# Attention with grouped queries on one core: K of group 1 by transposed load, VectorE's share of the exponentials from chunk 3 to 381, first chunks in two exponentials, other orders of loads and stores

## Chip, cores and metric

One core of a Trainium2 chip. Times are microseconds (us) of one execution on the device; the median of several is quoted. A "look" is the one execution of a run that was profiled; a "hole" is time in which TensorE starts no matmul though it has work left.

## The reference

```python
B, Hq, Hkv, Sq, Sk, D = 16, 32, 8, 288, 512, 128      # q, k, v in bf16, normal * 0.05
k = jnp.repeat(k, 4, axis=1); v = jnp.repeat(v, 4, axis=1)
scores = jnp.einsum("bhqd,bhkd->bhqk", q, k) * D ** -0.5
out = jnp.einsum("bhqk,bhkd->bhqd", softmax(scores), v)
```

A group is one KV head with its four query heads: 128 groups, each 4 x 288 = 1152 query rows (9 tiles of 128) against 512 keys (4 tiles). Its 4608 score columns are cut into three chunks of 1536: 384 chunks.

## The kernel before

For each chunk n, TensorE computes the scores S into one of two PSUM halves, ScalarE the exponential into one of six SBUF buffers, and two chunks later TensorE the product with V (PV); VectorE takes a reciprocal of the row sum and multiplies. In every sixth chunk 120 columns are "shared": VectorE computes their exponential itself by a polynomial, in eight operations spread over two iterations.

```python
FIRST = 2; FIRST_SHARED = 6; EVERY = 6; LAG = 2; UG = 4; NSLOT = 3    # 4 groups are a unit of K and V
def shared(n): return FIRST_SHARED <= n < NS - NC and (n - FIRST_SHARED) % EVERY == 0    # NS 384, NC 3
# TensorE
for n in range(NS):
    op_s(n)                       # waits for K, for Q, and for the exponential of chunk n - 2
    if shared(n): op_sy(n)        # the 120 columns, into a free corner of PSUM
    if n == 2: op_kt(1, range(NJ), 1)     # K of group 1: four transposes on TensorE
    if n >= LAG: op_pv(n - LAG)   # waits for V, exponentials, and VectorE's eviction of r - 2
# VectorE
for r in range(NS - 1):
    n = r + LAG
    op_rc(r)
    if shared(n): op_y(n)
    if shared(n - 1): op_yu(n - 1, 1); op_yu(n - 1, 2); op_yp(n - 1)
    op_ev(r)
    if shared(n): op_yb(n); op_ym(n); op_yu(n, 0)
# GpSimd: V from its landing buffer to the layout for TensorE, one copy per group
def op_vc(g):    # waits: V landed; s_pv >= 3 * (g - 2) + 2
    tensor_copy(v_sb[...], vd_sb[...])
# SyncE: loads of the start, in order; the rest is a list sorted by due times
first = [q(0), v(groups 0), q(1), k(groups 2..3), v(groups 1..3), q(2), q(3)]
# ScalarE issues K of group 0 and, when that is in place, K of group 1 (both plain, for TensorE's transposes)
```

## Time and profile before

| | us |
|---|---|
| time, median of 6 runs (521.55 to 522.85) | 521.69 |
| span of the profiled run | 519.98 |
| first exponential / end of the last | 5.05 / 516.47 |
| six chunks in the steady part | 7.98 |
| scores of chunk 6 begin / its Q landed | 12.39 / 11.37 |

The lines that carry the reading are in the prediction. A timeline line is: start, duration, engine, line of the kernel, operation, output<-input, shape, count, and in brackets the idle time before it and what ended it. PE is TensorE, DVE VectorE, ACT ScalarE, POOL GpSimd, SPq SyncE's issues. L439 or L449 is S, L479 or L489 is PV (the changed kernel's lines lie 10 lower). Matmul ends are modelled, so a hole is read from starts. "The clock is full" is read from starts too: 512-column matmuls start 0.427 apart before it and 0.216 after it.

### The profile page before, as it was taken

The page shows a single profiled execution, that of the slowest core. Times are in us where ns is not written, and L with a number is a line of the kernel's source. Part 1 is how long each engine was busy: PE and PEld are TensorE (multiplying, and loading weights), DVE is VectorE, ACT ScalarE, POOL GpSimd, SP SyncE. Part 2 cuts the span into 40 slices and gives each one's busy share as a digit, 9 for nine tenths or more (in the row PEclk, how much of TensorE's full clock was granted, in tenths as well). Part 3 has the DMA queues.
Part 4 walks back from the last instruction along what each step waited for, and adds up shares of the span by engine and source line. Part 5 has one row for each costly group of instructions (what it writes and reads, how often), then busy time and mean ns, then how long its engine had stood idle before and what let it go on. Part 6 is the DMA issues. An engine that isn't in the chain of part 4 may idle for free.

```text
span 520.0 us, 15243 instructions
## 1 busy us (share of the span) xinstructions
PE 510.3 (98%) x6118; PEld 394.6 (76%) x6224; DVE 369.6 (71%) x1315; ACT 513.3 (99%) x393; POOL 79.8 (15%) x135
## 2 busy tenths in 40 slices
PE   8999999999999999999999999999999999999997
PEld 5777777777777777777777777777777777777776
DVE  2767767777777677676776776767767767677776
ACT  7999999999999999999999999999999999999997
POOL 2111111111111111111111111111111111111110
PEclk9999999999999999999999999999999999999999
DMA  9999999999999998999999989999998989998212
GB/s 186 237 218 230 267 194 248 225 213 210 219 233 256 208 245 201 235 248 240 215 241 209 209 225 220 241 185 209 229 240 232 227 194 201 192 234 198 86 69 93
DMA packets 253078, 110.06 MB, mean 212 GB/s; under 512 B 219728, under 2 KB 236752, under 8 KB 253008
## 3 DMA queue, kind: packets, MB, share of 16 engines
q1 hardware_dynamic: 252720, 108.82, 97.7%
q8 instruction: 49, 0.80, 0.7%
q10 hardware_dynamic: 288, 0.26, 0.2%
q14 instruction: 21, 0.17, 0.2%
HBM read 17.04 MB, written 37.75 MB: 105 GB/s over the span
## 4 chain that ended last, share of the span: by engine, by line
ACT 98%; DMA 1%; issue 1%; DVE 0%; PE 0%
ACT pt_sb L516 97%; DMA qt_sb<-in_q_dram 1%; ACT pt_sb L511 1%; PE ps_s L439 0%; DVE o_sb L585 0%; DVE o_sb L595 0%; PE ps_s L479 0%; DVE rl_sb L575 0%; PE ps_o L669 0%; DVE bad_sb L621 0%; DVE flag_i L734 0%; DVE bad_sb L618 0%
## 5 line engine op out<-in xcount | busy, mean ns | idle before, releaser
L516 ACT ACTIVATE pt_sb<-ps_s 128x1536 bf16<-128x1536 f32 (+2 forms) x384 | 508.8, 1441 | 0.0
L479 PE MATMUL ps_o<-v_sb,pt_sb 128*128 128x129 bf16 x4584 | 322.3, 220 | 1.1
L479 PEld LDWEIGHTS ps_o<-v_sb,pt_sb 128*128 128x128 bf16 x4584 | 282.8, 98 | 49.7 <-DVE o_sb L585 14.1
L439 PE MATMUL ps_s<-qt_sb,kt_sb 128*128 128x512 bf16 (+2 forms) x1430 | 290.4, 320 | 5.0 <-DMA qt_sb<-in_q_dram 0.5
L585 DVE TENSOR_TENSOR o_sb<-ps_o,rl_sb 128x384 bf16<-128x384 f32 x382 | 211.9, 555 | 9.3 <-DVE rl_sb L575 0.5
L439 PEld LDWEIGHTS ps_s<-qt_sb,kt_sb 128*128 128x128 bf16 x1536 | 123.9, 98 | 62.3 <-issue 1.1
L575 DVE RECIPROCAL rl_sb<-ps_o 128x3 f32<-128x3 f32 x382 | 68.1, 178 | 125.5 <-PE ps_o L479 124.0
L568 POOL COPY v_sb<-vd_sb 128x512 bf16<-128x512 bf16 x128 | 78.8, 616 | 429.1 <-PE ps_o L479 408.9
L549 DVE SCALAR_TENSOR_TENSOR u_sb<-u_sb,m_sb 128x120 f32<-128x120 f32 x126 | 35.6, 283 | 2.2
L556 DVE SCALAR_TENSOR_TENSOR pt_sb<-u_sb,e_sb 128x120 bf16<-128x120 f32 x63 | 17.8, 283 | 2.2
L549 DVE SCALAR_TENSOR_TENSOR u_sb<-m_sb 128x120 f32<-128x120 f32 x63 | 17.4, 277 | 0.0
L527 DVE TENSOR_SCALAR y_sb<-ps_o 128x120 f32<-128x120 f32 x63 | 15.9, 253 | 0.0
L540 DVE TENSOR_SCALAR m_sb<-t_sb 128x120 int32<-128x120 int32 x63 | 14.1, 223 | 2.2
L540 DVE TENSOR_SCALAR e_sb<-t_sb 128x120 int32<-128x120 int32 x63 | 13.6, 216 | 0.0
L450 PE MATMUL ps_o<-qt_sb,kt_sb 128*128 128x120 bf16 x63 | 13.6, 216 | 0.0
L533 DVE TENSOR_SCALAR t_sb<-y_sb 128x120 int32<-128x120 f32 x63 | 13.4, 213 | 0.0
L450 PEld LDWEIGHTS ps_o<-qt_sb,kt_sb 128*128 128x128 bf16 x63 | 6.2, 98 | 7.4
L511 ACT ACTIVATE pt_sb<-ps_s 128x512 bf16<-128x512 f32 x6 | 3.3, 616 | 2.3 <-PE ps_s L439 2.3
L411 DVE COPY kt_sb<-ps_o 128x128 bf16<-128x128 bf16 (+2 forms) x3 | 1.0, 336 | 6.2 <-PE ps_o L404 6.1
L613 DVE TENSOR_REDUCE st_sb<-rl_sb 128x1 f32<-128x72 f32 (+1 forms) x16 | 3.5, 216 | 0.0
L611 DVE TENSOR_REDUCE st_sb<-rl_sb 128x1 f32<-128x72 f32 (+1 forms) x16 | 3.5, 216 | 0.0
L417 PE MATMUL ps_o<-const-bfloat16-1.0 128*128 128x512 bf16 (+1 forms) x6 | 2.4, 570 | 0.9 <-PEq L752 0.9
(32 smaller groups left out, 12.0 us busy)
## 6 DMA issues: line engine op xcount, KB each, us to landing
out_dram<-o_sb SPq DMA_DIRECT2D x127, 288.0 KB, 3.7
vd_sb<-in_v_dram SPq DMA_DIRECT2D x31, 512.0 KB, 5.5
qt_sb<-in_q_dram SPq DMA_TRANSPOSE x128, 4.9
kt_sb<-in_k_dram SPq DMA_TRANSPOSE x32, 5.1
vd_sb<-in_v_dram SPq DMA_DIRECT2D x1, 384.0 KB, 4.6
out_dram<-o_sb SPq DMA_DIRECT2D x3, 96.0 KB, 1.6
kd_sb<-in_k_dram ACTq DMA_DIRECT2D x2, 128.0 KB, 2.7
vd_sb<-in_v_dram SPq DMA_DIRECT2D x1, 128.0 KB, 3.3
```

The lines of the kernel that those rows point to most:

```text
L439: ins = emit(eng, w_x, lambda: eng.matmul(ps_s[:, n % 2, c:c + w], kt_sb[:, sl, j, gi, :], qg[:, t * P:t * P + w], start=True, stop=True))
L450: emit(eng, [("s_ev", n - LAG - 1)], lambda: eng.matmul(ps_o[:, (n - LAG) % 2, BANK - W:BANK], kt_sb[:, (g // UG) % NSLOT, j, g % UG, :], ...
L479: ins = emit(eng, w_x, lambda: eng.matmul(outs(r)[:, t - r % NC * TPC, :], pt(g, t, j), v_sb[:, sl, gi * NJ + j, 0:DV], start=(x == 0), st ...
L516: emit(eng, waits, lambda: eng.activation(d, s, ACTF.Exp, scale=scale)).then_inc(sem["s_e"], 1)
L527: emit(eng, [("s_yb", nth(n) - NB), ("s_pv", n - LAG + 1)], lambda: eng.tensor_scalar(out=y_sb[:, b], in0=ps_o[:, (n - LAG) % 2, BANK - W: ...
L533: emit(eng, [("s_ym", 2 * (nth(n) - NB)), ("s_y", nth(n))], lambda: eng.tensor_scalar(out=t_sb[:, b], in0=y_sb[:, b], scalar1=Y_MUL, scala ...
L540: emit(eng, [("s_yp", nth(n) - NB), ("s_yb", nth(n))], lambda: eng.tensor_scalar(out=dst[:, b], in0=t_sb[:, b], scalar1=mask, scalar2=bits ...
L549: lambda: eng.scalar_tensor_tensor(out=u_sb[:, b, x], in0=src, scalar=QUARTIC[x], in1=m, op0=ALU.add, op1=ALU.mult)
L556: lambda: eng.scalar_tensor_tensor(out=pt_sb[:, n % NPT, CH - W:CH], in0=u_sb[:, b, 2], scalar=QUARTIC[3], in1=e_sb[:, b].bitcast(FP32), o ...
L568: emit(eng, waits, lambda: eng.tensor_copy(v_sb[:, sl, gi * NJ:(gi + 1) * NJ, 0:D], vd_sb[:, sl, gi].rearrange("p (j d) -> p j d", d=D))). ...
L575: emit(eng, [("s_pv", r + 1)], lambda: eng.reciprocal(rl_sb[:, TPC * r:TPC * (r + 1)].unsqueeze(2), outs(r)[:, :, D:DV])).then_inc(sem["s_ ...
L585: emit(eng, waits, lambda: eng.tensor_tensor(out=o_sb[:, g % NO, t0:t0 + TPC, :], in0=outs(r)[:, :, 0:D], in1=rl_sb[:, TPC * r:TPC * (r + ...
```

## The change

Its intent: take the four transposes of K of group 1 off TensorE's start, relieve ScalarE earlier and once more at the end, and loosen the first and last steps.

```diff
-    FIRST = 2
-    FIRST_SHARED = 6
+    FIRST = 3
+    PARTS = {0: (1, 2, 3), 1: (2, 3), 2: (2, 3), NG * NC - 1: (1, 2, 3)}   # where exponentials are cut, in banks of 512
+    FIRST_SHARED = 3
+    FINE = NG - 2                                   # groups stored chunk by chunk (was: the last alone)
-            return FIRST_SHARED <= n < NS - NC and (n - FIRST_SHARED) % EVERY == 0
+            return FIRST_SHARED <= n < NS - 2 and (n - FIRST_SHARED) % EVERY == 0
-        first += [lambda: op_q(1), lambda: op_k(0, 2), lambda: op_v(0, None, 1, UG), lambda: op_q(2), lambda: op_q(3)]
+        first += [lambda: op_q(1), lambda: op_k(0, 1, 2), lambda: op_v(0, None, 1, 2), lambda: op_k(0, 2), lambda: op_v(0, None, 2, UG), lambda: op_q(2), lambda: op_q(3)]
-            sp.append((t, lambda u=u: op_k(u)))
-            sp.append((t + (2.0 if u >= NSLOT else 0.35), lambda u=u: op_v(u)))
+            sp.append((t + (0.35 if u == 1 else 0), lambda u=u: op_k(u)))
+            sp.append((t + (2.0 if u >= NSLOT else 0 if u == 1 else 0.35), lambda u=u: op_v(u)))
-                if n == 2:
-                    op_kt(1, range(NJ), 1)
-            op_kd(eng, 1)                                # on ScalarE, after a wait
-            op_kc(1, range(NJ), 1, 3)                    # on VectorE
```

More of the change, by code (lines that the diff above doesn't have):

```diff
@@ L205, in bass_standalone__gqa_softmax__near_ridge_kernel @@
             S("s_k%d" % i)
-        for name in ["s_v0", "s_v1", "s_s0", "s_y", "s_yb", "s_ym", "s_yu", "s_yp", "s_kd0", "s_kd1", "s_id", "s_kp"]:
+        for name in ["s_v0", "s_v1", "s_v2", "s_s0", "s_y", "s_yb", "s_ym", "s_yu", "s_yp", "s_kd0", "s_id", "s_kp"]:
             S(name)
@@ L224, in choose @@
             if key == "sp":
-                for (s, n) in need(eng, [("s_ol", 16 * (NC + 1))]):
+                for (s, n) in need(eng, [("s_ol", 16 * NC * (NG - FINE))]):
                     eng.wait_ge(s, n)
@@ L238, in bass_standalone__gqa_softmax__near_ridge_kernel @@
         qt_sb = main.enter_context(nc.sbuf_tensor("qt_sb", [P, NQ, NT, P], BF16))
-        kd_sb = main.enter_context(nc.sbuf_tensor("kd_sb", [P, 2, NJ * D], BF16))
+        kd_sb = main.enter_context(nc.sbuf_tensor("kd_sb", [P, NJ * D], BF16))
         ident = main.enter_context(nc.sbuf_tensor("ident", [P, P], BF16))
@@ L278, in emit, with op_kd, op_k @@
             return ins
-        def op_kd(eng, g):
-            eng.dma_start(kd_sb[:, g], kd_v[:, g]).then_inc(sem["s_kd%d" % g], 16)
-        def op_k(u, g0=0):
+        def op_kd(eng):
+            eng.dma_start(kd_sb[:], kd_v[:, 0]).then_inc(sem["s_kd0"], 16)
+        def op_k(u, g0=0, g1=UG):
             eng = nc.sync
@@ L291, in op_k @@
             eng.dma_start_transpose(
-                kt_sb[:, sl, :, g0:UG].rearrange("d j g p -> d j (g p)"),
-                k_v[(u * UG + g0) * P:(u + 1) * UG * P]
-            ).then_inc(sem["us_k%d" % sl if u > 0 else "s_k2"], 16)
+                kt_sb[:, sl, :, g0:g1].rearrange("d j g p -> d j (g p)"),
+                k_v[(u * UG + g0) * P:(u * UG + g1) * P]
+            ).then_inc(sem["us_k%d" % sl if u > 0 else "s_k%d" % g0], 16)
         def op_v(u, eng=None, g0=0, g1=UG):
@@ L326, in have @@
             if u == 0 and kind == "k":
-                return ("s_k%d" % min(g, 2), (2, 1, 16)[min(g, 2)])
+                return ("s_k%d" % min(g, 2), (2, 16, 16)[min(g, 2)])
             if u == 0:
-                return ("s_v%d" % min(g, 1), 16)
+                return ("s_v%d" % min(g, 2), 16)
             return ("us_%s%d" % (kind, u % NSLOT), 16 * (u // NSLOT + (0 if u % NSLOT == 0 else 1)))
@@ L336, in op_store @@
                     eng.wait_ge(s, n)
-                eng.dma_start(o_v[g], o_sb[:, g % NO].rearrange("p t d -> p (t d)")).then_inc(
-                    sem["s_o%d" % (g % NO) if g < LASTG - 1 else "s_ol"], 16)
+                eng.dma_start(o_v[g], o_sb[:, g % NO].rearrange("p t d -> p (t d)")).then_inc(sem["s_o%d" % (g % NO)], 16)
             else:
-                for (s, n) in need(eng, [("s_ev", NC * g + i + 1)] + ([("s_ea", 1)] if i == NC - 1 else [])):
+                for (s, n) in need(eng, [("s_ev", NC * g + i + 1)] + ([("s_ea", 1)] if (g, i) == (LASTG, NC - 1) else [])):
                     eng.wait_ge(s, n)
@@ L346, in stored @@
         def stored():
-            return [("s_o%d" % (g % NO), 16 * (g // NO + 1)) for g in range(NG - NO, LASTG - 1)]
+            return [("s_o%d" % (g % NO), 16 * (g // NO + 1)) for g in range(NG - NO, FINE)]
         def op_stored():
@@ L372, in used, with part, ahead @@
             return max(b for b in range(NC) for t in range(b * TPC, (b + 1) * TPC) for j in range(NJ) if place(t, j)[0] == i)
+        def part(n, x):
+            return sum(x >= e for e in PARTS.get(n, (TPC,)))
+        def ahead(n):
+            return sum(len(PARTS[m]) - 1 for m in range(n))
         def ready(n, x):
-            if n < FIRST and x < TPC - 1:
-                return ("s_eb", n * (TPC - 1) + x + 1)
-            return ("s_e", n + 1 + (x if n == NS - 1 else 0))
+            p = part(n, x)
+            if n < FIRST and p < len(PARTS[n]) - 1:
+                return ("s_eb", ahead(n) + p + 1)
+            return ("s_e", n + 1 + (p if n == NS - 1 else 0))
         def sequence(b):
@@ L397, in pt, with op_kt @@
             return pt_sb[:, (g * NC + i) % NPT, c:c + P]
-        def op_kt(g, tiles, bank):
+        def op_kt(tiles, bank):
             eng = nc.tensor
@@ L403, in op_kt, with op_kc @@
             for x, j in enumerate(tiles):
-                ins = emit(eng, [("s_id", 2), ("s_kd%d" % g, 16)], lambda: eng.transpose(
-                    dst[:, x * P:(x + 1) * P], kd_sb[:, g, j * D:(j + 1) * D], ident[:]))
+                ins = emit(eng, [("s_id", 2), ("s_kd0", 16)], lambda: eng.transpose(
+                    dst[:, x * P:(x + 1) * P], kd_sb[:, j * D:(j + 1) * D], ident[:]))
             ins.then_inc(sem["s_kp"], 1)
-        def op_kc(g, tiles, bank, n):
+        def op_kc(tiles, bank, n):
             eng = nc.vector
@@ L411, in op_kc @@
             emit(eng, [("s_kp", n)], lambda: eng.tensor_copy(
-                kt_sb[:, 0, tiles[0]:tiles[-1] + 1, g], src)).then_inc(sem["s_k%d" % g], 1)
+                kt_sb[:, 0, tiles[0]:tiles[-1] + 1, 0], src)).then_inc(sem["s_k0"], 1)
         def op_warm(n, w, dst):
@@ L440, in op_s @@
                     ps_s[:, n % 2, c:c + w], kt_sb[:, sl, j, gi, :], qg[:, t * P:t * P + w], start=True, stop=True))
-                if n < FIRST and (c + w) % BANK == 0 and c + w < CH:
+                if n < FIRST and (c + w) % BANK == 0 and (c + w) // BANK in PARTS[n][:-1]:
                     ins.then_inc(sem["s_s0"], 1)
@@ L507, in op_exp @@
                 parts = [(0, CH - W)]
-            if n < FIRST or n == NS - 1:
-                parts = [(x, x + BANK) for x in range(0, CH, BANK)]
+            if n in PARTS:
+                parts = [(x * BANK, y * BANK) for (x, y) in zip((0,) + PARTS[n], PARTS[n])]
             for x, (c, e) in enumerate(parts[:-1]):
-                ins = emit(eng, [("s_s0", (TPC - 1) * n + x + 1)] if n < FIRST else waits, lambda: eng.activation(
+                ins = emit(eng, [("s_s0", ahead(n) + x + 1)] if n < FIRST else waits, lambda: eng.activation(
                     d[:, c:e], s[:, c:e], ACTF.Exp, scale=scale))
@@ L636, in bass_standalone__gqa_softmax__near_ridge_kernel @@
             sp.append((t, lambda g=g: op_q(g)))
-        for g in range(LASTG):
+        for g in range(FINE):
             sp.append((NC * (g + 1) + LAG + 1.5, lambda g=g: op_store(g)))
-        for r in range(NC * LASTG, NS):
+        for r in range(NC * FINE, NS):
             sp.append((r + LAG + 2.6, lambda r=r: op_store(r // NC, r % NC)))
@@ L655, in _ @@
             op_warm(1, P, ps_o[:, 1])
-            op_kt(0, range(1), 0)
-            op_kt(0, range(1, NJ), 1)
+            op_kt(range(1), 0)
+            op_kt(range(1, NJ), 1)
             op_warm(1, P, ps_s[:, 1])
@@ L675, in _ @@
         def _(eng):
-            op_kd(eng, 0)
+            op_kd(eng)
             eng.activation(dum[:], nc.const_aps.tensor(0.0, [P, 1], FP32), ACTF.Exp)
-            for (s, n) in need(eng, [("s_k0", 2)]):
-                eng.wait_ge(s, n)
-            op_kd(eng, 1)
             for n in range(NS):
@@ L699, in _ @@
             eng.memset(one_f[:], 1.0)
-            op_kc(0, range(1), 0, 1)
-            op_kc(0, range(1, NJ), 1, 2)
-            op_kc(1, range(NJ), 1, 3)
+            op_kc(range(1), 0, 1)
+            op_kc(range(1, NJ), 1, 2)
             per_b = G * NC
```

## The prediction

> **What bounds the kernel now.** I read the page's busy row and its slices first, then the chain of waits, then the timeline of TensorE alone at the start and in the middle, then that of ScalarE, and last the landings of the first transfers.
>
> ```profile
> PE 510.3 (98%) x6118; PEld 394.6 (76%) x6224; DVE 369.6 (71%) x1315; ACT 513.3 (99%) x393; POOL 79.8 (15%) x135
> ACT 98%; DMA 1%; issue 1%; DVE 0%; PE 0%
> ```
>
> Two engines are full: ScalarE (the exponentials) and TensorE. The chain names ScalarE for 98%, but it follows an engine back as long as that engine has no recorded gap, so it cannot choose between two full engines. The timeline of TensorE can. Here it is in the middle of the run (start, duration, engine, line, operation; L439 are the scores S of one chunk, L479 the product with V of one chunk, PV):
>
> ```profile
> 494.04 0.82 PE L439 MATMUL ps_s<-qt_sb,kt_sb 128*128 128x512 bf16 x6
> 494.69 0.84 PE L479 MATMUL ps_o<-v_sb,pt_sb 128*128 128x129 bf16 x12
> 495.37 0.81 PE L439 MATMUL ps_s<-qt_sb,kt_sb 128*128 128x512 bf16 x3
> 496.02 0.84 PE L479 MATMUL ps_o<-v_sb,pt_sb 128*128 128x129 bf16 x12
> ```
>
> S of six matmuls takes 494.69 - 494.04 = 0.65, S of three 496.02 - 495.37 = 0.65, PV 495.37 - 494.69 = 0.68 (12 x 57 ns). No time is left between them. A chunk costs 0.65 + 0.68 = 1.33 us, and with the third decimals of the trace's starts (1.328, 1.328 and 1.335 for the three chunks of a group) six chunks cost 7.982. The chain's pieces "ACT pt_sb L516 x6" start at 21.28, 29.26, 37.25, 45.23: 7.98 apart. So the period is the sum of the TensorE work, and the matmul starts show no hole after 13.5 us that isn't a missing record, up to 515.7.
>
> ScalarE is only just faster. One exponential of 1536 columns moves the end of the one before by 1.343 us (7.929 + 1.507 = 9.436, 9.260 + 1.519 = 10.779, 10.591 + 1.532 = 12.123, 11.924 + 1.542 = 13.466), one of 512 columns by 0.489, so 63 ns fixed and 0.833 ns a column; the 1416 columns of a shared chunk by 1.243. Six chunks, one of them shared: 5 x 1.343 + 1.243 = 7.96 against TensorE's 7.98. Without sharing it would be 8.06 and ScalarE the bound. That is how it is before the first shared chunk, number 6:
>
> ```profile
> 4.41 2.91 PE L439 MATMUL ps_s<-qt_sb,kt_sb 128*128 128x512 bf16 x12 [0.46 <-DMA qt_sb<-in_q_dram]
> 7.31 0.40 PE L404 MATMUL ps_o<-ident,kd_sb 128*128 128x128 bf16 x4
> 7.54 0.84 PE L479 MATMUL ps_o<-v_sb,pt_sb 128*128 128x129 bf16 x12
> 8.31 0.81 PE L439 MATMUL ps_s<-qt_sb,kt_sb 128*128 128x512 bf16 x3
> 8.96 0.94 PE L479 MATMUL ps_o<-v_sb,pt_sb 128*128 128x129 bf16 x12
> ...
> 13.04 0.88 PE L479 MATMUL ps_o<-v_sb,pt_sb 128*128 128x129 bf16 x12
> ```
>
> The holes of TensorE: 0.15 before 7.31 (K of group 1 lands at 7.26), 0.23 for its four transposes, 0.09 before 8.31 (VectorE's copy of them, 7.74 to 8.16), 0.10 inside the PV of chunk 1 (0.94 in place of 0.84: its last four matmuls wait for the exponential of chunk 2), 0.04 inside the PV of chunk 4 (waits for chunk 5's exponential, end 13.466, restart 13.521: 55 ns from end to use). After that it never waits. The time is thus: ScalarE from its first exponential at 5.05 to about 13.5, TensorE to about 512, ScalarE again to 516.5 (no shared chunk after 378), and the tail.
>
> **What the Trainium skill says.** "TensorE: Matmul & The Clock Gate", section "Wait — 56ns, not 53.3ns?": warm matmuls start 55.6 ns apart at 128 columns and 215.7 at 512. The trace agrees: 57 ns at 129 columns, 0.65 / 3 = 216. The same page under "Back-to-back issue gap" expects about 81 ns per 128-column matmul in a stream with weight loads; this trace has 57 in such a stream, and I use that. "DMA: Bandwidth & Descriptors", section "Issuing engines are not separate DMA queues": transfers of all engines run on the same 16 DMA engines, another issuer saves only issue time. So K of group 1 moves from one issuer to another without being fewer bytes. "Perfetto Trace Analysis", section "DVE / Act Engine Instruction (TENSOR_ADD, Activation, etc)": the window reported runs until the write is acknowledged. That is why durations of 1.51 stand at starts 1.33 apart, and why I count with ends.
>
> **The change part by part.**
>
> *K of group 1 by transposed load.* Removes 0.15 + 0.23 + 0.09 = 0.47 us of TensorE's holes and work. When does it land? It is issued after Q of group 1, where K of groups 2 and 3 stood (4.21, landed 8.30 behind Q at 6.70 and the other K at 7.26). At half that size I estimate 7.2 to 7.7. PV of chunk 0 can begin when S of chunk 2 ends, 7.155, and S of chunk 3 at 7.155 + 0.68 = 7.84, so the load is hidden. TensorE then stands 0.47 earlier (7.84 for 8.31).
>
> *Chunks 1 and 2 in two exponentials.* 3 + 2 + 2 instructions where there were 3 + 3 + 1: the sum on ScalarE doesn't change. Ends by my costs: chunk 0 at 6.622, chunk 1 at 7.539 and 8.028, chunk 2 at 8.945 and 9.434 (before: 9.436). The split lets PV of chunk 1 go on at 8.945 + 0.055 = 9.00 and not at 9.49; another hole goes. ScalarE gains nothing.
>
> *VectorE's share from chunk 3.* Chunk 3 ends at 9.434 + 1.243 = 10.677 (before 10.779), 4 at 12.02, 5 at 13.363, 6 (not shared now) at 14.706, 7 at 16.049, 8 at 17.392 (before 17.398: one share each by then). TensorE needs the exponential of the next chunk for the last four matmuls of every third PV. PV of chunk 4 would get there at 13.18 and waits until 13.363 + 0.055 = 13.42 (before 13.52: 0.10 gained). PV of chunk 7 gets there after 3 chunks, 3.99, at 17.43 (a restart costs 0.01) and waits until 17.392 + 0.055 = 17.447; before it got there at 13.521 + 3.991 = 17.512 without a wait. So of nearly 0.5 us only 17.512 - 17.447 = 0.065, say 0.05 with the restart, is left: ScalarE gives the rest away, because it starts at the same 5.05 and has as much to do. From chunk 9 on it has another share and TensorE is the bound, at the same 7.98 for six chunks.
>
> *The end.* Chunk 381 is shared too: ScalarE could be 0.10 earlier, but S of chunk 382 starts at 512.66 and its last matmul is ready 0.85 later, 513.52, and the exponential starts now at 513.53. Gain 0.02 to 0.03. VectorE's extra six operations (about 1.4 us by the 0.22 to 0.28 us of each) lie in its gaps.
>
> *Stores of group 126 by chunk.* The last store, issued at 517.83, needs group 127's last chunk; the stores before it landed by 518.9. It doesn't wait for them. 0.
>
> *V of unit 1 ahead of its K, and two more issues.* K of unit 1 now lands last of three transfers. In the kernel before it landed at 16.4, Q of group 4 at 17.3, V at 19.4; in the new order I estimate K at 19.4 to 20.1. S of chunk 12 wants it at 20.3. V had until about 21.7 (one POOL copy of 0.62 before PV of chunk 12 at 22.4). So 0 if it lands in time; the margin falls from 4 us to under 1.
>
> The sum is -0.05 - 0.03 = -0.08 us, plus a chance of a new wait on a load, which I put at one in three with 0.1 to 0.5 us: some +0.1 in the mean. From the median of 521.83 (the profiled run took 521.67) that is **521.7 us**.
>
> **The rivals.**
> (1) *TensorE keeps all of the start's gain*: -0.4 us, 521.3. For it: the holes are real and TensorE is the bound for 97% of the time. Against it: ScalarE's ends above; for this, exponentials would have to follow each other in 1.33 (spacing of starts) and not 1.343 (spacing of ends), which would make chunk 8 end some 0.1 earlier.
> (2) *A load becomes the wait.* Two issues more, 1.3 and 0.6 us on SyncE's queue, stand before Q of group 2. It landed at 11.37; S of chunk 6 wants it at 12.08. Going from transposed to plain loads seems to cost the queue some 0.5 us (the window table shows dips), and the new order alternates more. A wait there or at chunk 12 isn't won back, as TensorE has no slack: +0.1 to +0.6, 521.9 to 522.3.
> (3) *The share at the start comes too early*: VectorE's chain for chunk 3 (rows L527 to L556, some 2.4 us with what lies between) would hold up PV of chunk 4. It begins at about 9.3 and is done by 11.9, PV of chunk 4 starts at 12.7: no.
>
> **Range and chances.** All terms are under 0.6 us, 0.1% of the time, and the three runs before spread over 1.3. So the range comes from that spread and rival 2 above, rival 1 below: 521.1 to 522.4. Nothing can make 2%, which is 10 us, unless the period of six chunks changes, and no part of the change touches what fills it.
>
> **What would show it right or wrong.** Right: no transposes at 7.3, S of chunk 3 at 7.84, the exponential of chunk 3 still at 9.26, PV of chunk 4 and, by little, of chunk 7 with a wait inside, then six chunks in 7.98 to the end. Wrong at the load: S of chunk 3, 6 or 12 starting late with a DMA as its releaser. Wrong at ScalarE: S of chunk 12 more than 0.2 us before 20.36. Wrong at the end: less or more than 3.5 us from the last exponential's end to the span's end.

## More of the kernel before

S of chunk 6 in the kernel before, with no hole ahead of it:

```profile
11.71 0.84 PE L479 MATMUL ps_o<-v_sb,pt_sb 128*128 128x129 bf16 x12
12.39 0.76 PE L439 MATMUL ps_s<-qt_sb,kt_sb 128*128 128x512 bf16 x3
```

## The result, and the profile after

| | before | changed |
|---|---|---|
| median (6 runs each) | 521.69 (521.55 to 522.85) | 522.24 (521.90 to 522.45) |
| span of the profiled run | 519.98 | 520.42 |
| scores of chunk 6 begin / its Q landed | 12.39 / 11.37 | 12.57 / 12.52 |
| V of group 8 copied at | 34.31 | 35.20 |

The ratio is 1.0007 (0.9994 to 1.0020), 0.55 us slower by the medians. That interval is about 0.7 us to either side, and of the runs below only experiments 4 and 10 and the held-back ones differ from the kernel before by more than theirs: what carries the argument are the steps in the traces, not the medians. A ratio is the mean time of one kernel's fast runs over that of the other's in the same rounds, so not quite the ratio of the medians quoted.

The page's busy row and chain of the changed kernel, to be held against those in the prediction:

```profile
PE 510.4 (98%) x6115; PEld 394.3 (76%) x6221; DVE 371.2 (71%) x1322; ACT 513.5 (99%) x393; POOL 79.5 (15%) x135
PE 95%; DVE 1%; issue 1%; SPq 1%; DMA 1%
```

The sums are the same to 0.5%; only the chain has changed its name, from ScalarE to TensorE, which shows how little that name says where two engines are full. Where the 0.45 us of the spans lie is found by laying the two traces side by side by one instruction that comes once a chunk, VectorE's reciprocal. For chunk 7 it starts at 17.95 before and 18.10 after (+0.15), for chunk 22 at 37.91 and 38.37 (+0.46), for chunk 383 at 517.16 and 517.59 (+0.43). So there are two losses, one before chunk 7 and one about chunk 20, a small gain at the end, and 480 us with no difference at all.

The first loss, in the timeline of TensorE in the changed kernel:

```profile
7.73 0.76 PE L449 MATMUL ps_s<-qt_sb,kt_sb 128*128 128x512 bf16 x3
8.38 0.98 PE L489 MATMUL ps_o<-v_sb,pt_sb 128*128 128x129 bf16 x12
...
11.35 1.02 PE L489 MATMUL ps_o<-v_sb,pt_sb 128*128 128x129 bf16 x12
12.57 0.82 PE L449 MATMUL ps_s<-qt_sb,kt_sb 128*128 128x512 bf16 x3 [0.20 <-DMA qt_sb<-in_q_dram]
```

The transposes are gone and S of chunk 3 starts at 7.73 in place of 8.31. By 12.2 the PV of chunk 3 is through (its last matmul starts at 12.15), but S of chunk 6 starts at 12.57: it waits for Q of group 2. The profile's 0.20 is from a modelled end; by the starts the hole is 0.36.

The second loss, in the timeline of the changed kernel around 36 us, GpSimd and VectorE beside TensorE:

```profile
35.20 0.67 POOL L578 COPY v_sb<-vd_sb 128x512 bf16<-128x512 bf16 x1 [4.48 <-DMA vd_sb<-in_v_dram]
35.31 0.69 DVE L559 SCALAR_TENSOR_TENSOR u_sb<-m_sb 128x120 f32<-128x120 f32 x1
...
36.87 0.55 DVE L595 TENSOR_TENSOR o_sb<-ps_o,rl_sb 128x384 bf16<-128x384 f32 x1
...
37.48 0.17 PEld L489 LDWEIGHTS ps_o<-v_sb,pt_sb 128*128 128x128 bf16 x3 [0.63 <-DVE o_sb L595]
```

An operation of VectorE that takes 0.28 in every other shared chunk takes 0.69 here, and ends at 36.00, just after the copy that GpSimd began at 35.20 (to 35.87). Everything behind it on VectorE is 0.4 late, among it the eviction of chunk 20 at 36.87, on which the PV of chunk 22 waits: it starts at 37.48, 0.31 late by the starts (the "hole at chunk 20" of what follows). The chain of waits of this stretch leads back through VectorE's whole polynomial, not through ScalarE.

Why just here? GpSimd's copy for group g is released by PV of chunk 3g - 5. The old phase of sharing (n = 6, 12, ...) put VectorE's chain beside the copies of odd groups, the new one (n = 3, 9, ...) beside those of even groups. The first group of every unit, 4, 8, 12, ..., is even, and only its copy can be held up by the load of V. A copy on time runs beside the reciprocal, the clamp y and the eviction, which read PSUM: in the kernel before all 63 clamps overlap a copy and still take 0.253. A copy that is late runs into the polynomial, which reads SBUF.

The Trainium skill has this in "SBUF — State Buffer", section "SBUF: two separate sides": VectorE and GpSimd share one port pair, an exclusive lock. GpSimd's operations take it, and of VectorE's those with two inputs in SBUF or in a "2-port perf mode"; whichever starts first holds it for its whole instruction and the other "fully blocks". The traces agree: 0.69 for 0.28 here, ending 0.13 after the copy, and all 63 hits of experiment 4 end 0.13 after theirs. Which mode an operation with one input ran in, no trace here shows.

### The profile page after: what moved, and what is told of

Read it like the earlier page. It is cut to its first block, busy times and chain, and to the rows that moved or that the text cites. A ratio compares the mean times of both kernels' runs of the same rounds, so it can differ in the third digit from the quotient of the medians.

```text
span 520.4 us, 15250 instructions
## 1 busy us (share of the span) xinstructions
PE 510.4 (98%) x6115; PEld 394.3 (76%) x6221; DVE 371.2 (71%) x1322; ACT 513.5 (99%) x393; POOL 79.5 (15%) x135
## 4 chain that ended last, share of the span: by engine, by line
PE 95%; DVE 1%; issue 1%; SPq 1%; DMA 1%
PE ps_o L489 50%; PE ps_s L449 44%; DMA qt_sb<-in_q_dram 1%; PE ps_o L460 1%; SPq L293 0%; DVE o_sb L595 0%; DVE u_sb L559 0%; SPq L304 0%; SPq L318 0%; SPq L313 0%; DVE rl_sb L585 0%; DVE pt_sb L566 0%; DVE m_sb L550 0%; DVE t_sb L543 0%; DVE o_sb L605 0%
## 5 line engine op out<-in xcount | busy, mean ns | idle before, releaser
L489 PEld LDWEIGHTS ps_o<-v_sb,pt_sb 128*128 128x128 bf16 x4584 | 282.7, 98 | 50.2 <-DVE o_sb L595 14.2
L550 DVE TENSOR_SCALAR m_sb<-t_sb 128x120 int32<-128x120 int32 x64 | 14.3, 223 | 2.2
L550 DVE TENSOR_SCALAR e_sb<-t_sb 128x120 int32<-128x120 int32 x64 | 13.9, 217 | 0.0
L521 ACT ACTIVATE pt_sb<-ps_s 128x512 bf16<-128x512 f32 (+1 forms) x6 | 4.3, 748 | 2.3 <-PE ps_s L449 2.3
```

The lines of the kernel that those rows point to most:

```text
L489: ins = emit(eng, w_x, lambda: eng.matmul(outs(r)[:, t - r % NC * TPC, :], pt(g, t, j), v_sb[:, sl, gi * NJ + j, 0:DV], start=(x == 0), st ...
L550: emit(eng, [("s_yp", nth(n) - NB), ("s_yb", nth(n))], lambda: eng.tensor_scalar(out=dst[:, b], in0=t_sb[:, b], scalar1=mask, scalar2=bits ...
```

## The experiments

**1 to 4: the two losses one by one, together, and the second 63 times over.**

Experiment 1, the changed kernel with

```diff
-lambda: op_v(0, None, 2, UG), lambda: op_q(2), lambda: op_q(3)
+lambda: op_q(2), lambda: op_v(0, None, 2, UG), lambda: op_q(3)
```

> The changed kernel with Q of group 2 issued before V of groups 2 and 3. In the changed kernel the scores of chunk 6 started at 12.57 because Q of group 2 landed at 12.52; without that wait TensorE would be there at about 12.2. Theory (two separate losses, the load at 12.5 us and VectorE's stalled operation at 35 us): Q lands by 12.0, the scores of chunk 6 start at 12.15 to 12.3, the step of 0.3 us at chunk 20 stays, time 521.9 to 522.0 (0.25 to 0.3 below the changed kernel's 522.24). Rival (the late Q only takes up slack that ScalarE's chain would take anyway): start of chunk 6 moves, but the time stays at 522.2.

Measured 522.50 (521.85 to 522.85; the kernel before beside it 521.85). Q landed at 11.37 and nothing waited for it. But S of chunk 6 started at 13.00: TensorE's clock came to full at 8.2 us in this look (4.9 in that of the changed kernel) and the first three chunks of scores ran at half speed. The hole at chunk 20 stayed, 0.24, with a VectorE operation of 0.57 beside the copy. Here it was one with a single input (L550, 0.22 when alone). So the look confirms the cause of the second loss. Of the first it shows only that Q lands earlier: at 13.00 even the old landing of 12.52 would have been in time. The expected gain in time isn't there. The five runs spread over 1.0: the two fastest took 521.85 and 521.89, the look was one of the other three (522.50 to 522.85).

Experiment 2, the changed kernel with

```diff
-    FIRST_SHARED = 3
+    FIRST_SHARED = 6
```

> The changed kernel with the first shared chunk at 6 and not at 3 (63 shared chunks, the phase of before). Theory (in the new phase VectorE's chain meets GpSimd's late copy of V of group 8): the copy at 35 us is as late as before, but the VectorE operation of 0.69 us is gone, TensorE has no hole at 37 us, and the time is 521.9 to 522.0, 0.3 below the changed kernel. The wait for Q at 12.5 stays. Rival (the hole at 37 us comes from the late V alone): the hole of 0.3 us stays with the new phase, 522.2 to 522.35.

GpSimd and VectorE of this kernel in the same stretch of the timeline:

```profile
35.28 0.18 DVE L585 RECIPROCAL rl_sb<-ps_o 128x3 f32<-128x3 f32 x1 [0.56 <-PE ps_o L489]
...
35.50 0.56 DVE L595 TENSOR_TENSOR o_sb<-ps_o,rl_sb 128x384 bf16<-128x384 f32 x1
...
35.97 0.61 POOL L578 COPY v_sb<-vd_sb 128x512 bf16<-128x512 bf16 x1 [5.36 <-DMA vd_sb<-in_v_dram]
...
36.62 0.18 DVE L585 RECIPROCAL rl_sb<-ps_o 128x3 f32<-128x3 f32 x1 [0.56 <-PE ps_o L489]
```

The copy came even later than in the changed kernel (35.97), nothing of VectorE was stretched and TensorE has no hole there: the late V alone costs nothing, the phase makes it cost. Q of group 2 landed at 12.25, just early enough for S of chunk 6 at 12.40. The profiled run took 521.63, like the kernel before (521.67 in its look), and its last reciprocal is 0.06 behind that of the kernel before. The median of five, 522.12, is not lower by the 0.3 expected; what the other four runs lost no profile shows.

Experiment 3, experiment 1's edit and V of unit 2 ahead of its K:

```diff
-            sp.append((t + (0.35 if u == 1 else 0), lambda u=u: op_k(u)))
-            sp.append((t + (2.0 if u >= NSLOT else 0 if u == 1 else 0.35), lambda u=u: op_v(u)))
+            sp.append((t + (0.35 if u <= 2 else 0), lambda u=u: op_k(u)))
+            sp.append((t + (2.0 if u >= NSLOT else 0), lambda u=u: op_v(u)))
```

> The changed kernel with both causes taken away by order alone: Q of group 2 before V of groups 2 and 3, and V of unit 2 before its K (sharing from chunk 3 stays). Theory: no wait at 12.5, V of group 8 there before its copy is due at 34 us, no stalled VectorE operation, no hole at 37 us: 521.45 to 521.65, at or 0.1 to 0.2 below the kernel before (521.69). Rival (other parts of the change cost something too): stays above 521.8.

Measured 522.18 (521.87 to 522.68). In the look the copy for group 8 came on time (35.04, released by TensorE), every operation of VectorE there took its usual time, and after 14.2 us TensorE never waited until the end. Both losses are gone, and yet the time isn't better: the clock came to full at 9.0 us, and S of chunk 6 started at 13.33. The edit also made a new collision: V of groups 2 and 3 now lands behind Q, and the copy of group 2 ran into the polynomial of chunk 3 (0.57 for 0.28; the line merges it with the next operation), so that PV of chunk 4 started 0.18 late:

```profile
12.43 0.89 DVE L559 SCALAR_TENSOR_TENSOR u_sb<-u_sb,m_sb 128x120 f32<-128x120 f32 x2
12.53 0.65 POOL L578 COPY v_sb<-vd_sb 128x512 bf16<-128x512 bf16 x1 [3.64 <-DMA vd_sb<-in_v_dram]
...
14.15 0.68 PEld L489 LDWEIGHTS ps_o<-v_sb,pt_sb 128*128 128x128 bf16 x12 [0.51 <-DVE o_sb L595]
```

The "rival" of the expectation isn't excluded by the time alone.

Experiment 4, the kernel before with each copy of V released one chunk later:

```diff
-                waits.append(("s_pv", NC * (g - 2) + 2))
+                waits.append(("s_pv", NC * (g - 2) + 3))
```

> The kernel before with each GpSimd copy of V released one chunk later, so that it falls on VectorE's two-input operations of the shared chunk. Measures the disputed cost by itself, 63 times over. Theory (a copy on GpSimd and a VectorE operation with two inputs in SBUF shut each other out): those operations go from 0.28 to 0.6 to 0.7 us, TensorE waits about 0.3 us for each shared chunk, time +10 to +20 us. Rival (the long operation at 35 us had another cause, or TensorE has slack for it): durations stay at 0.28, time within 1 us.

Measured 534.04 against 521.85, ratio 1.0233 (1.0218 to 1.0249). Two of this kernel's groups on VectorE (after the bar: busy us in all, mean ns of one):

```profile
L549 DVE SCALAR_TENSOR_TENSOR u_sb<-u_sb,m_sb 128x120 f32<-128x120 f32 x126 | 53.7, 426 | 2.2
L549 DVE SCALAR_TENSOR_TENSOR u_sb<-m_sb 128x120 f32<-128x120 f32 x63 | 17.4, 277 | 0.0
```

And the line of its waits for what PV waits on (us in total, times, longest):

```profile
PEld ps_o L479 <- DVE o_sb L585: 32.1, 63, 0.5
```

In the group that is hit there are two operations a shared chunk, at a mean of 426 ns in place of 283: one of the two is hit, 0.57 long, and the whole chain 0.29 later. The other group isn't hit and keeps its 277. The time grew by 12.2 / 63 = 0.19 us a collision: the rest is slack. In the kernel before the weight load of PV waits 14.1 us in all, 63 times, for the same eviction, which costs nothing as its matmuls are still busy; here 32.1. That a copy on GpSimd stretches these operations, and what that costs, is shown.

**5 to 8: the start held back, to take the clock out.** Dummy exponentials on ScalarE (20, of 512 columns each) pace dummy matmuls on TensorE, and SyncE and the load of K start when 16 of them are done:

```diff
+            for k in range(1, 21):            # TensorE, ahead of the first transposes
+                for x in range(1 if k <= 10 else 2): matmul(ps_o[:, 1], ones, ones)   # waits for the k-th dummy exponential
+            eng.wait_ge(sem["s_pad"], 16)     # SyncE, ahead of its first load
```

(Condensed; the dummies' buffers, their exponentials and the same wait ahead of ScalarE's load of K are cut.)

> The first looks showed a second thing that differs between executions: TensorE's clock goes to full at 4.9 us (changed kernel), 6.0 (before) or 8.2 and later (experiments 1 and 3), and a late clock delays the start whatever the kernel. This is the kernel before with that taken out: loads and first scores are held back by some 10 us, in which TensorE does dummy matmuls and ScalarE dummy exponentials, so that the clock is full when the first scores begin; the order and spacing of the loads after that is as before. It is the base for the three that follow. Expected: full clock well before the first scores, time about 531.5, and a smaller spread than the 0.7 us that the kernel before has beside experiments 1 to 4; 514.9 us from the first exponential to the end of the span, as in the kernel before.

> The changed kernel with the same held-back start. Theory (its loss comes from the late Q of group 2 and from the stalled VectorE operation at chunk 20): 0.3 to 0.6 us above the held-back kernel before, with both waits in the trace. Rival (the difference of 0.5 us came from when the clock went to full): within 0.15 of the held-back kernel before, or below it.

> The kernel before with K of group 1 by transposed load alone (and V of groups 1 to 3 in two loads, as the changed kernel has it), sharing from 6 as before, held-back start. Theory: the wait for Q of group 2 alone, scores of chunk 6 at 0.1 to 0.3 later than in the held-back kernel before, no stalled VectorE operation: +0.1 to +0.3 us. Rival (the load costs nothing): within 0.1.

> Experiment 3 (changed kernel, Q of group 2 before V of groups 2 and 3, V of unit 2 before its K) with the held-back start. Unheld it stayed at 522.18, above what I expected, with a clock that came full only at some 8.9 us. Theory (the late clock was why): 0.1 to 0.25 below the held-back kernel before. Rival (another part of the change costs): at or above it.

| held back | median (range) | S of chunk 6 after the first exponential | from there |
|---|---|---|---|
| kernel before | 533.41 (532.97 to 534.81) | 9.17 | nothing |
| changed | 531.83 (531.67 to 533.21) | 7.61 | a wait for K of unit 1 of 1.2, hole at chunk 20 of 0.35 |
| K of group 1 alone | 532.36 (532.25 to 533.28) | 7.65 | nothing |
| changed, both orders | 531.90 (531.32 to 532.27) | 7.21 | hole of 0.1 before chunk 12, a wait for K of unit 2 of 0.9 |

The clock was full at 3.9 to 5.8 us (read from the modelled lengths of the dummies, 0.63 and then 0.39), long before the first scores at 14.4, so that worked; as a base it failed. The chain of waits of the held-back kernel before shows where it loses:

```profile
14.58 4.55 DMA kd_sb<-in_k_dram
19.13 0.05 issue
19.18 0.40 PE ps_o L408 x4
```

K of group 1, issued by ScalarE, took 4.55 us to land and not 2.99. In the kernel before it is issued 0.06 us after SyncE's transposed K of groups 2 and 3, here 0.55 after it. It isn't a fair base for the other three, and my expectations against it are void. That the order of two issuers made K of group 1 late isn't shown: Q of group 1, issued before both, also took 5.03 us to land and not 3.84.

The three others compare among themselves: with Q first, S of chunk 6 begins 0.40 us earlier (7.21 for 7.61), the size of the first loss, and 0.30 of that is left at chunk 9. With the clock full in both, this is the plainest test of the first loss. The medians don't follow, as V of unit 2 ahead of its K made that K late. Nor do the looks stand for the medians: those of the changed kernel and of the two orders are the slowest of their five runs. The time of K of group 1 alone is too high: it has the fault told under experiment 10, and its end, from the last reciprocal on, took 3.46 us where the three others took 2.78 to 2.83.

**9 to 12: parts alone in the kernel before, and a mended version.**

Experiment 9, the kernel before with the change's sharing:

```diff
-    FIRST_SHARED = 6
+    FIRST_SHARED = 3
-            return FIRST_SHARED <= n < NS - NC and (n - FIRST_SHARED) % EVERY == 0
+            return FIRST_SHARED <= n < NS - 2 and (n - FIRST_SHARED) % EVERY == 0
```

> The kernel before with the change's sharing alone (chunks 3, 9, ..., 381 in place of 6, 12, ..., 378). Theory: -0.05 to -0.1 us from the start and -0.03 from the end, so 521.6; but the phase now meets the copies of V of the groups 4, 8, 12, which come when their load has landed, and if one of them overlaps a two-input VectorE operation there is a hole of TensorE of about 0.3 and the time is 521.9. Rival (the new phase is harmless by itself): no long VectorE operation after chunk 3 and 521.6 in all runs.

Measured 522.16 (522.02 to 522.45; before 521.72), so slower by 0.44, and not for the reason given. Group 8 was harmless (its copy 0.2 late). The main loss is at the PV of chunk 4:

```profile
10.31 1.17 POOL L568 COPY v_sb<-vd_sb 128x512 bf16<-128x512 bf16 x2 [4.65 <-DMA vd_sb<-in_v_dram]
10.52 0.48 DVE L533 TENSOR_SCALAR t_sb<-y_sb 128x120 int32<-128x120 f32 x1
11.04 0.52 DVE L540 TENSOR_SCALAR m_sb<-t_sb 128x120 int32<-128x120 int32 x1
...
13.35 0.51 PEld L479 LDWEIGHTS ps_o<-v_sb,pt_sb 128*128 128x128 bf16 x9 [0.79 <-DVE o_sb L585]
```

V of groups 1 to 3 lands in one piece at 10.26, GpSimd copies two groups at once, and both copies lie on the polynomial of chunk 3 (0.48 and 0.52 for 0.21 and 0.22); TensorE has a hole of 0.46. A second hole, 0.18 before PV of chunk 10, comes from the copy of group 4, which V of unit 1 made late: it began at 19.62 and stretched an operation to 0.57. In the changed kernel V of group 1 lands by itself at 8.17 and is copied at 8.22. So the split of V, which looked like a detail, takes the copy of group 1 out of the way; that of group 2 can still hit (experiment 3).

Experiment 10, the changed kernel with all but the transposed load of K of group 1 (and the split loads) put back:

```diff
-    FIRST = 3; PARTS = {0: (1, 2, 3), 1: (2, 3), 2: (2, 3), NG * NC - 1: (1, 2, 3)}; FIRST_SHARED = 3; FINE = NG - 2
+    FIRST = 2; PARTS = {0: (1, 2, 3), 1: (1, 2, 3), NG * NC - 1: (1, 2, 3)}; FIRST_SHARED = 6; FINE = NG - 1
     # sharing up to NS - NC again, and K of unit 1 ahead of its V
```

> The kernel before with K of group 1 by transposed load alone (V of groups 1 to 3 in two loads; sharing, exponentials, other orders as before), not held back. Theory: the scores of chunk 6 wait for Q of group 2 and the step in TensorE's stream at chunks 3 to 6 is 0.15 to 0.3 over the kernel before: 521.85 to 522.0. Rival (this part is neutral or a gain): 521.75 or less.

Measured 522.72 (522.37 to 522.97). My edit had a fault: it also left group 126's store among those that SyncE waits for before the last three, so the end, from the last reciprocal on, took 3.63 us in place of 2.82. The time is therefore 0.8 too high; less that, it would be some 521.9, an estimate. The trace before the end says more: Q of group 2 landed at 12.83, S of chunk 6 started at 12.88, and from chunk 9 on TensorE stood 0.58 further behind its first exponential than in the kernel before, with no loss at chunk 20. The transposed load with its split loads alone brings the first loss.

Experiment 11, the kernel before with two more shared chunks, and the numbering of VectorE's buffers to match:

```diff
-            return FIRST_SHARED <= n < NS - NC and (n - FIRST_SHARED) % EVERY == 0
+            return (n == 3 or n == NS - 3 or 6 <= n < NS - NC and (n - 6) % EVERY == 0)
```

> The kernel before with two more shared chunks, 3 and 381, and 6 to 378 kept, so that the steady phase stays as before. Theory: ScalarE's start is relieved by 0.1 us and nothing collides: -0.1 to -0.15, 521.55 to 521.6. Rival (ScalarE isn't what limits the start): 521.7.

Measured 522.43: the theory fell. Chunk 3 meets the two copies as in experiment 9 (a hole of 0.35 before 13.5 us, where the shared scores of chunk 6 wait for VectorE), while the end is no worse: sharing 381 makes the reciprocal of chunk 381 0.26 later, but that is made up, and at the last reciprocal the kernel is 0.50 behind the kernel before, after 0.48 at chunk 7.

Experiment 12, the changed kernel with the edits of experiments 1 and 11 and the order of unit 1 put back:

```diff
-            sp.append((t + (0.35 if u == 1 else 0), lambda u=u: op_k(u)))
-            sp.append((t + (2.0 if u >= NSLOT else 0 if u == 1 else 0.35), lambda u=u: op_v(u)))
+            sp.append((t, lambda u=u: op_k(u)))
+            sp.append((t + (2.0 if u >= NSLOT else 0.35), lambda u=u: op_v(u)))
```

> The changed kernel with Q of group 2 before V of groups 2 and 3, K of unit 1 before its V as in the kernel before, and shared chunks 3, 6, 12, ..., 378, 381. Theory: no wait at chunk 6, no collision, K of unit 1 in time: 521.45 to 521.6, at or below the kernel before. Rival (something in the changed kernel costs that I haven't found): 521.9 or more, with no step in TensorE's stream to account for it.

Measured 521.72 (521.45 to 521.91), the kernel before beside it 521.72 (521.47 to 521.96), ratio 1.0001 (0.9987 to 1.0015). Q landed at 11.59, nothing waited for a load, no collision at chunk 20 although its copy was 1.0 late, and S of chunk 6 at 12.27, with the clock full at 6.3. It takes the changed kernel's loss away and beats neither the kernel before nor its own estimate. Against the kernel before its TensorE is 0.09 ahead from chunk 4 on and its last reciprocal 0.06; as its first exponential came 0.18 earlier (4.87 for 5.05), the changed start has gained nothing that can be seen.

The looks together (4, 9 and 11, the kernel before with single edits, left out):

| kernel | clock full | Q of group 2 landed | S of chunk 6 | hole at chunk 20 |
|---|---|---|---|---|
| before | 6.0 | 11.37 | 12.39 | 0 |
| changed | 4.9 | 12.52 | 12.57 | 0.31 |
| 1, Q first | 8.2 | 11.37 | 13.00 | 0.24 |
| 2, phase of before | 6.3 | 12.25 | 12.40 | 0 |
| 3, Q first and V first | 9.0 | 11.22 | 13.33 | 0 |
| 10, K of group 1 alone | 4.7 | 12.83 | 12.88 | 0 |
| 12, mended | 6.3 | 11.59 | 12.27 | 0 |

In the changed order Q landed at 12.25 to 12.83, with Q first or in the old order at 11.05 to 11.6. The clock differs from execution to execution, though all kernels have the same dummy matmuls ahead; that is why looks can't be compared by their time, but by their steps.

## Why the prediction was right or wrong

- *The bound.* Right: TensorE's sum sets the steady part; six chunks take 7.98 in every kernel without collisions.
- *K of group 1.* Right: landed at 7.34 (estimate 7.2 to 7.7), S of chunk 3 at 7.73 (7.84).
- *ScalarE gives the rest away.* Right in kind: the exponential of chunk 3 starts 4.21 us after the first one, as before. I named only the waits of PV of chunk 4 and 7, and neither came, because the late Q had held TensorE back; PV of chunk 3 waits (0.17), for the exponential of chunk 4. The working had a wait only in every third PV; the PV ahead of that one needs the next chunk as well.
- *The end.* Right: the last reciprocal won 0.04 over chunk 22's lag (0.02 to 0.03 predicted). The stores of group 126 cost and gave nothing visible: from the last exponential's end to the span's end 3.53, before 3.51.
- *The sum, -0.08.* Without the two losses it would be +0.43 - 0.29 - 0.31 = -0.17, of which 0.05 is a first exponential that came earlier by chance. The 0.29: S of chunk 6 could have started at 12.21, and the wait of PV of chunk 4 for an exponential, 0.06, would then have come back. It is an estimate: experiment 12, with neither loss, is 0.06 ahead at its last reciprocal, less than its earlier first exponential gives.
- *The chance of a wait on a load, "one in three".* This term was mis-sized. Rival 2 named the very load, but I worked out a landing for K only. With that order Q came too late for TensorE in four looks of five (changed, experiment 10, held-back changed and held-back K alone; experiment 2 just escaped). K of unit 1, the other load named, landed at 19.89 (estimate 19.4 to 20.1) and was in time; in the held-back changed kernel TensorE waited 1.2 for it.
- *"No part of the change touches what fills" the period.* This step failed. The first shared chunk sets which of GpSimd's copies lie beside VectorE's chain. I looked for the cost of sharing on VectorE, TensorE and ScalarE, and didn't ask what else uses VectorE's way to SBUF at that time. It cost 0.31 once, because only V of unit 2 was late enough. No rival and no term held this loss: that 522.24 lies in the range is in part luck, as the range was wide enough for rival 2, and only about half of the loss is rival 2's (0.29 beside 0.31).
- *Rival 3, "no".* True of the changed kernel, where the polynomial of chunk 3 was hit once (0.58 for 0.28) without harm, but for a reason I hadn't seen: experiment 9 shows 0.46 when V isn't split, and experiment 3 0.18 when it is.

**What stays open.** Experiments 1 to 3 took away what their profiles show and their medians stayed at 522.1 to 522.5, while experiment 12 came back to 521.72. Their looks 1 and 3 had a clock full only after 8 us. Whether the kernel before loses as much with such a clock no look shows, and how often it happens neither. A difference between 1 to 3 and 12 is the order of unit 1: with V first, SyncE's issue of K of unit 1 took 4.3 to 5.8 us (four unheld looks), with K first 2.2 to 3.2 (six looks). In looks 1 and 3 it made TensorE wait for no load. But with V first K of unit 1 landed only 0.3 to 0.7 before its use in the four unheld looks (2.4 in that of experiment 12), and in the held-back changed kernel TensorE waited 1.2 for it; that it was late in some of the runs without a profile is a rival that nothing here excludes.

## What to carry to other kernels

When an engine's stream has no holes left, ask of a change not what it saves but what it moves in time: each load's landing against the first use, and each operation's neighbours on the other engines. A periodic piece of work has a phase; shifting it by half a period changes no sum and can bring it beside another engine's irregular work. And with a start that differs between executions, compare traces by steps, at an instruction that comes once a round, before believing medians that differ by 0.1%.

## What the Trainium skill lacked or had wrong

- "SBUF — State Buffer" has the lock and it holds here. It gives no price for it in a pipeline: a 0.61 us copy stretched 120-column VectorE operations from 0.28 to 0.57 to 0.69, also ones with a single SBUF input (0.22 to 0.52 and 0.57), and cost 0.19 us of the end time for each collision in experiment 4. Those with two inputs ended 0.13 after the copy, those with one 0.07. Operations reading PSUM were not touched (0.253).
- "TensorE: Matmul & The Clock Gate" gives the change to the full clock as some 4 us into sustained activity, plus or minus 0.5. The start here isn't sustained: the matmuls of all unheld looks began at 0.86 and paused for about 0.7 before the scores, and the change came between some 4 us (experiment 9) and 9.0. In the two latest looks (8.2 and 9.0) it came 3.6 and 4.5 after the scores began, which fits the page; it has no figure for a start with a pause.
- The same page, under "Back-to-back issue gap", expects 81 ns per 128-column and 131 ns per 512-column matmul in a stream with weight loads; this one runs at 57 and 216.
- "DMA: Bandwidth & Descriptors" calls the time that a sequencer needs to start a transfer usually small beside the transfer. SyncE's issue of one transposed load of four groups (K of unit 1) took 2.2 to 5.8 us of the 6.0 to 7.8 from its start to its landing, and everything behind it in the queue waited.
- No page gives landing times for short loads behind one another: a transposed load of 288 KB landed 3.4 to 5.4 us after its issue among the first four of each unheld look.
